# A planned kernel: a conversion leaves GpSimd, transfers on two queues are charged for each other, and sums in place go to the DMA queue

## The chip, the cores and the metric

The kernel runs on one core of a Trainium2 chip. The metric is the device time of one execution in microseconds; lower is better. The core has five engines with an instruction queue each: TensorE (PE, with its weight loads as PEld), VectorE (DVE), ScalarE (ACT), GpSimd (POOL) and SyncE (SP). In this kernel SP issues plain loads and stores, and POOL issues the transfers that add to their destination.

## The reference, cut to what matters

```
x = causal softmax attention of q, k, v     (2 batches, 12 heads, 448 rows, 64 columns)
h = x @ w_in    (896 x 768 @ 768 x 2048);  g = h * clip(h + 3, 0, 6) / 6;      y = g @ w_out
h = y @ w_in2                            ;  g = max(h, 0) + alpha * min(h, 0); out = g @ w_out2
```

Everything is float32 at the ends. The weights arrive as 64-bit words of float64.

## The kernel before, in words

**Arithmetic.** Each of the four large products is a Strassen form: seven block products where eight would be usual. A float32 product is made of three fp32r matmuls of 448 columns, from a high and a low part of each operand (`three`, L578). A layer has 168 such threes in `w_in` and 168 in `w_out`, so there are 672 in all, and `three` gives each of them a due time in the order of the program: 146.2 us plus 0.608 us for each one before it.

**Preparing operands.** `convert` turns one 768 KB load (`raw`) into 768 float32 columns: L249 on ACT takes the high words, a second pass (`lowest`) takes three low bits out of a byte, and L262 on DVE joins them. The second pass runs on ACT (L259), or, where `help` is set, on ACT or on POOL (L256). `help` is set for the first `HELP = 5` pairs of `w_in`. `split` (L275 to L284) and `both` (L612, L613) make the high part on ACT and the low part on DVE. Under `help` a split of attention's results may also go to POOL.

**Sums in place.** `add_on` adds one tile to another. It is either one DVE instruction (L303) or one DMA with an accumulating write issued by POOL (L301). There are 104 of them: in `w_in` two of 384 columns for each of 16 pairs; in `w_out` for each layer 12 of 768 columns (`onto`: four each for products 7, 6 and 3) and 24 of 448 columns (`add_g`: eight each for products 7, 6 and 4). The products of `w_out` run in the order 1, 2, 7, 6, 4, 5, 3. Sums for product 6 need those of product 7 to have been split, and those for 4 need the sums of 6.

**The order of the work** is found by a planner while the program is built (`Plan.solve`). It simulates the five queues with a cost for each operation, takes at each step the operation with the earliest due time among those that can start first, and writes the result out as a fixed order for each engine. Each engine then works strictly in that order, so one instruction that waits holds up everything behind it. A due time is worked back from the due times of the matmuls that need the result. An operation with two possible engines goes to the one that the planner thinks will be done first. A transfer is modelled by `lands(wait, us)`: it lands `us` after the later of its own wait and the transfer before it on the same queue (`landed[e]`). The two queues, SP's and POOL's, don't see one another. `raw` has three buffers, `ends` two, the weights' class `w` 20. `SEEDS` drive a random change of attention's due times; `SEND = 1` fixes one of the two sums of each `w_in` pair (the one into `w2`) on POOL.

**Stages.** Attention runs to about 90 us with the first preparation of weights beside it, then come `w_in` and `w_out` of layer 0, and from about 300 us those of layer 1.

Of the kernel before, what the change touches and what calls it, by code (L numbers as in the profile page):

```python
# [13 lines left out]
U8, U16, F16 = mybir.dt.uint8, mybir.dt.uint16, mybir.dt.float16  # L14
AF = mybir.ActivationFunctionType
ALU = mybir.AluOpType
# [6 lines left out]
PAIRS = KFF // 2  # L23
# [9 lines left out]
PE, DVE, ACT, POOL, SP = "PE", "DVE", "ACT", "POOL", "SP"  # L33


def f32(t):
    return t.bitcast(F32)
# [23 lines left out]

ISSUE, WAIT = 0.9, 4.2

TURN = {("r", "r"): 0.05, ("r", "t"): 0.17, ("r", "c"): 0.2, ("r", "q"): 0.15, ("r", "m"): 0.15, ("t", "r"): 0.12,
        ("t", "c"): 0.12, ("t", "q"): 0.1, ("m", "c"): 0.2, ("m", "r"): 0.1, ("m", "q"): 0.1}
LAG = {PE: 0.20, DVE: 0.12, ACT: 0.15, POOL: 0.10, SP: 0.04}
FAR = 1.0e6


class Plan:
# [3 lines left out]

    def op(self, on, emit, reads=(), writes=(), due=FAR, chain=None, also=(), port=False, mode=None):

# [24 lines left out]
    def solve(self, slots, strict, overlay, vary=0, seeds=()):  # L103
# [9 lines left out]
        bias = dict.fromkeys(LAG, 0.5)  # L113
        both = {o: o.on for o in self.ops[:vary]}
        hold = 0.01
        for i, seed in enumerate(seeds):
# [3 lines left out]
            if not i:  # L120
                hold = rng.choice((0.01, 0.05, 0.1, 0.2, 0.3, 0.5))
                bias = {e: rng.choice((0.0, 0.2, 0.5, 1.0, 2.0, 4.0)) for e in LAG}
# [9 lines left out]
        first = {}  # L132
        for o in self.ops:
            for b in o.bufs:
                if b.cls in strict:
                    first[b] = min(first.get(b, (FAR, 0)), (o.due, o.index))
        queue = {c: sorted((b for b in first if b.cls == c), key=first.get) for c in strict}
        waiting = {o: len(o.before) for o in self.ops}
        ready = {e: [] for e in LAG}
        clock, landed, port = dict.fromkeys(LAG, 0.7), dict.fromkeys(LAG, 0.0), 0.0  # L140

        def put(o):
            o.ready = {}
# [8 lines left out]
        while len(done) < len(self.ops):  # L152
            best = None
            room = {c: queue[c][:len(free[c])] for c in strict}
            for e in LAG:
                can = []
                for o in ready[e]:
                    t = max(clock[e] + TURN.get((mode, o.mode), 0.0) if e == PE else clock[e], o.ready[e])
                    if (e == POOL and e not in o.dma) or (e == DVE and o.port):
                        t = max(t, port)  # L160
                    ok = True
                    need = {}
                    for b in o.bufs:
                        if b.slot is None:
                            need[b.cls] = need.get(b.cls, 0) + 1
                            f = free[b.cls]
                            if len(f) < need[b.cls] or (b.cls in room and b not in room[b.cls]):
                                ok = False
                                break
                            t = max(t, sorted(f)[need[b.cls] - 1][0])  # L170
                    if ok and len(o.on) > 1:
                        def done_by(x, us):
                            late = max(clock[x], o.ready[x], port if (x == POOL and x not in o.dma) or (x == DVE and o.port) else 0.0)
                            return late + us + (bias[x] if x != o.on[0][0] else 0.0) + (sum(o.load) if x in o.dma else 0.0)

                        ok = e == min(o.on, key=lambda c: done_by(*c))[0]
                    if ok:
                        can.append((t, o))
                if can:
                    soon = min(can, key=lambda r: r[0])[0] + hold  # L180
                    t, o = min((r for r in can if r[0] <= soon), key=lambda r: (r[1].due, r[1].index))
                    key = (round(t, 2), o.due)
                    if best is None or key < best[0]:
                        best = (key, e, o, t)
            if best is None:
                raise RuntimeError("no step is possible: %s" % [
                    (e, o.on, [b.name for b in o.bufs]) for e in LAG for o in sorted(ready[e], key=lambda o: o.due)[:4]
                ])
            _, e, o, t = best
            for x, _ in o.on:  # L190
                ready[x].remove(o)
            o.eng, o.start = e, t
            mode = o.mode if e == PE else mode
            o.out = o.end = clock[e] = t + dict(o.on)[e]
            if (e == POOL and e not in o.dma) or (e == DVE and o.port):
                port = o.end
            if o.load and e in o.dma:
                first, us = o.load
                o.out = landed[e] = max(o.start + first, landed[e]) + us
            for b in [b for b in o.bufs if b.slot is None]:  # L200
                f = free[b.cls]
                k = min(range(len(f)), key=lambda i: f[i][0])
                b.slot = f.pop(k)[1]
                if b.cls in strict:
                    queue[b.cls].remove(b)
            for b in o.bufs:
                b.left -= 1
                b.end = max(b.end, o.out + LAG[e])
                if not b.left:
                    free[b.cls].append((b.end, b.slot))  # L210
            if any(b.cls in over_of for b in o.bufs):
                over_left -= 1
                over_end = max(over_end, o.end)
                if not over_left:
                    n = slots[over_cls]
                    free[over_cls] += [(over_end, n + i) for i in range(over_n)]
            for s in o.after:
                waiting[s] -= 1
                if not waiting[s]:
                    put(s)  # L220
            done.append(o)
# [3 lines left out]
class Kernel:  # L225
# [6 lines left out]

    def convert(self, src, sign=1.0, help=False, halves=False):

        nc, op = self.nc, self.plan.op
        raw = Buf("raw", "raw", 2 * DM, U32)
        w = Buf("w", "wf", DM, U32)
        ends = Buf("ends", "ends", DM, U32)  # L240
        keys = [(w, 0), (w, W3)] if halves else [w]

        def words(k):
            return raw.tile.rearrange("p (n two) -> p n two", two=2)[:, :, k]

        op((SP, 0.45), lambda e: nc.sync.dma_start(out=raw.tile, in_=src), writes=[(raw, "l"), (raw, "h")]).lands(2.3, 1.9)


        op((ACT, 0.80), lambda e: nc.scalar.activation(  # L249
            f32(w.tile), f32(words(1)), AF.Prelu, scale=sign * 2.0 ** -112, alpha=-2.0 ** 32), reads=[(raw, "h")], writes=keys)  # L250

        def lowest(e):
            byte = raw.tile.bitcast(U8).rearrange("p (n eight) -> p n eight", eight=8)[:, :, 3]
            if e == POOL:
                out = ends.tile.bitcast(U8).rearrange("p (n four) -> p n four", four=4)[:, :, 0]
                nc.gpsimd.tensor_scalar(out, byte, 1.0 / 32.0, 7.0, ALU.mult, ALU.min)  # L256
            else:
                out = ends.tile.bitcast(U16).rearrange("p (n two) -> p n two", two=2)[:, :, 0]
                nc.scalar.activation(out, byte, AF.Copy, bias=-0.4999, scale=1.0 / 32.0)  # L259

        op([(ACT, 0.93), (POOL, 0.95)] if help else (ACT, 0.93), lowest, reads=[(raw, "l")], writes=[ends])
        op((DVE, 0.87), lambda e: nc.vector.scalar_tensor_tensor(  # L262
            out=w.tile, in0=w.tile, scalar=3, in1=ends.tile.bitcast(U32), op0=ALU.logical_shift_left, op1=ALU.bitwise_or),
           reads=[ends], writes=keys, port=True)
        return w
# [29 lines left out]
    def add_on(self, out, cols, dst, src, reads, writes, send=False):  # L295

        nc = self.nc

        def emit(e):
            if e == POOL:  # L300
                nc.gpsimd.dma_start(out=dst(), in_=src(), accum_op=ALU.add)  # L301
            else:
                nc.vector.tensor_add(dst(), dst(), src())  # L303

        on = [(POOL, ISSUE), (DVE, 0.065 + 0.00105 * cols)]
        self.plan.op(on[:1] if send else on, emit, reads=reads, writes=writes, port=True).lands(WAIT, 0.0024 * cols, on=POOL)

    def copy(self, out, src, key, cols, sign=1.0):
        nc = self.nc
# [275 lines left out]

    def w_in(self, layer, m, src, due):
        nc, op = self.nc, self.plan.op
        help = layer * PAIRS + m < HELP
        w1 = self.convert(src[m], -1.0, help, True)
        w2 = self.convert(src[m + PAIRS], 1.0, help, True)  # L590
        s12 = Buf("w", "s12", DM, F32)
        left, right = slice(0, W3), slice(W3, DM)

# [1 line left out]
           reads=[(w2, 0), (w2, W3)], writes=[(s12, W3)], port=True)  # L595
        op((DVE, 0.47), lambda _: nc.vector.tensor_add(s12.tile[:, left], s12.tile[:, right], f32(w1.tile[:, left])),  # L596
           reads=[(s12, W3), (w1, 0)], writes=[(s12, 0)], port=True)
# [28 lines left out]
        a, b, c = Buf("ps", "a"), Buf("ps", "b"), Buf("ps", "c")  # L626
# [191 lines left out]
OVER = 38  # L818
WARM = 3
SPLIT = (0, 1)  # L820
HELP = 5
SEND = 1
SCALERS = 2
SEEDS = (16, 37982, 36857, 48248, 70450, 88331, 82478, 34058)
ATT = {"kq": 2 * S, "v": 8 * D, "e": 3 * P, "el": 4 * P, "small": 21, "a": 16 * P}


# [111 lines left out]
```

## Time and profile before

| What | us |
| --- | --- |
| median of three runs (523.89 to 526.14) | 523.96 |
| the profiled execution, its own time | 522.8 |
| its span, first to last instruction | 520.9 |
| busy: PE, DVE, ACT, POOL | 497.1 (95%), 448.0 (86%), 392.3 (75%), 117.3 (23%) |

The profile is of one execution on the one core. PE's busy time counts pipelined matmuls with modelled ends, so idle PE time in a stage is read from windows of that stage. A wait is put down to the releaser that came last. "Granted clock" is the share of TensorE's full clock that it was given.

### The profile page before, as it was taken

Reading aid. Unit: us, or ns where it says so; the run is one execution under the profiler, and the core shown is the slowest. Engines: PE = TensorE matmul, PEld = TensorE weight load, DVE = VectorE, ACT = ScalarE, POOL = GpSimd, SP = SyncE. Lnnn points to the kernel's source line nnn. Section 1 sums busy time; section 2 is a strip of 40 time slices with the busy share of each in tenths; the row PEclk is TensorE's granted clock in tenths of the full one; section 3 lists DMA queues with packets and bytes.
Section 4 is the critical chain, followed back from the end, with each engine's and each line's share of the span. In section 5 each row is a group of like instructions: output and inputs, shape, how many; then the busy total and the mean of one; then the engine's idle time right before and its main releaser. Section 6 shows DMA issues by size and latency. Waiting matters only on the chain. (4 is left out here: it accounts for less than half of the span.)

```text
span 520.9 us, 7558 instructions
## 1 busy us (share of the span) xinstructions
PE 497.1 (95%) x2598; PEld 428.7 (82%) x2598; DVE 448.0 (86%) x855; ACT 392.3 (75%) x746; POOL 117.3 (23%) x161
## 2 busy tenths in 40 slices
PE   8899999999799999997999999999999999879997
PEld 4666677788699999996999887999999999669996
DVE  6899998999699698988999999999879898699810
ACT  5999999687688798877875578888779997567201
POOL 2885687341100000351000001000000026010000
PEclk9999999999899999998999999999999999999999
DMA  8773115376654447899113255544446669930111
GB/s 276 271 240 110 52 42 182 94 208 160 171 147 138 170 140 246 205 227 250 30 57 94 108 137 155 152 136 137 137 137 185 200 196 227 205 61 1 53 54 53
DMA packets 23462, 76.10 MB, mean 146 GB/s; under 512 B 2688, under 2 KB 11264, under 8 KB 23424
## 3 DMA queue, kind: packets, MB, share of 16 engines
q1 hardware_dynamic: 15216, 61.76, 35.1%
q0 software_dynamic: 8208, 13.86, 15.3%
q8 instruction: 20, 0.33, 0.3%
q14 instruction: 18, 0.15, 0.1%
HBM read 59.00 MB, written 2.75 MB: 119 GB/s over the span
## 5 line engine op out<-in xcount | busy, mean ns | idle before, releaser
L259 ACT ACTIVATE ends<-raw 128x768 uint16<-128x768 uint8 x58 | 62.5, 1087 | 12.5 <-DMA raw<-w2o 4.3
L262 DVE SCALAR_TENSOR_TENSOR wf<-wf,ends 128x768 uint32<-128x768 uint32 x64 | 59.9, 953 | 12.6 <-ACT wf L249 12.5
L301 POOL DMA_DIRECT2D wf<-wf x24 | 21.0, 876 | 191.8 <-ACT ends L259 57.8
L249 ACT ACTIVATE wf<-raw 128x768 f32<-128x768 f32 x64 | 57.3, 904 | 2.0 <-DVE w3l L281 1.1
L301 POOL DMA_DIRECT2D g<-g x33 | 29.9, 1065 | 121.8 <-DVE g L657 29.0
L446 ACT ACTIVATE e<-e,small 128x384 f32<-128x384 f32 (+2 forms) x72 | 36.0, 505 | 7.3 <-DVE small L441 7.1
L441 DVE CUSTOM_DVE_ANT_0 e<-s,mask 128x384 f32<-128x384 f32 (+2 forms) x72 | 26.9, 417 | 4.3 <-PE s L490 4.2
L470 POOL TENSOR_SCALAR e<-e,small 128x128 f32<-128x128 f32 (+2 forms) x55 | 25.8, 486 | 8.2 <-DVE small L463 4.9
L313 ACT COPY o<-ya 128x448 f32<-128x448 f32 x3 | 1.6, 533 | 31.1 <-PE ya L578 31.1
L559 PE MATMUL o<-a,v 128*64 128x448 f32 (+3 forms) x192 | 23.4, 386 | 1.3 <-DVE small L441 0.9
L559 PEld LDWEIGHTS o<-a,v 128*64 128x64 f32 x192 | 12.5, 136 | 14.4 <-issue 4.6
L612 ACT CAST a1h<-wf 128x768 fp32r<-128x768 f32 x16 | 13.3, 833 | 11.8 <-DVE wf L262 11.8
L612 ACT CAST s<-wf 128x384 fp32r<-128x384 f32 x32 | 16.1, 511 | 8.1 <-DMA wf<-wf 8.1
L613 DVE TENSOR_TENSOR s<-wf,s 128x384 fp32r<-128x384 f32 x32 | 17.2, 552 | 5.4 <-ACT s L612 5.3
L256 POOL TENSOR_SCALAR ends<-raw 128x768 uint8<-128x768 uint8 x6 | 20.3, 3378 | 5.8 <-DVE wf L262 5.6
L490 PE MATMUL s<-kq 64*128 64x384 f32 (+2 forms) x144 | 20.5, 401 | 0.6 <-DMA kq<-kq 0.6
L515 PE MATMUL t<-ident,e 128*128 128x128 f32 x144 | 19.6, 279 | 1.5 <-POOL e L470 0.6
L490 PEld LDWEIGHTS s<-kq 64*128 64x128 f32 x144 | 13.3, 190 | 8.1 <-issue 3.6
L515 PEld LDWEIGHTS t<-ident,e 128*128 128x128 f32 x144 | 15.6, 141 | 4.5 <-POOL e L470 3.0
L612 ACT CAST s12h<-s 128x768 fp32r<-128x768 f32 x16 | 13.4, 836 | 7.6 <-DVE s L596 7.6
L613 DVE TENSOR_TENSOR s12l<-s,s12h 128x768 fp32r<-128x768 f32 x16 | 15.3, 955 | 2.7 <-PE a L578 2.1
L663 DVE SCALAR_TENSOR_TENSOR g<-r,alpha,g 128x448 f32<-128x448 f32 x24 | 16.3, 680 | 0.3 <-ACT r L661 0.3
(838 smaller groups left out, 1790.2 us busy)
## 6 DMA issues: line engine op xcount, KB each, us to landing
raw<-w1i SPq DMA_DIRECT2D x16, 768.0 KB, 5.7
raw<-w1o SPq DMA_DIRECT2D x16, 768.0 KB, 5.4
raw<-w2i SPq DMA_DIRECT2D x16, 768.0 KB, 4.7
raw<-w2o SPq DMA_DIRECT2D x16, 768.0 KB, 5.8
g<-g POOLq DMA_DIRECT2D x33, 224.0 KB, 7.0
kq<-kq SPq DMA_DIRECT2D x11, 448.0 KB, 5.9
v<-v SPq DMA_DIRECT2D x12, 256.0 KB, 2.7
wf<-wf POOLq DMA_DIRECT2D x16, 192.0 KB, 3.0
```

The source lines that it names most:

```text
L249: op((ACT, 0.80), lambda e: nc.scalar.activation(f32(w.tile), f32(words(1)), AF.Prelu, scale=sign * 2.0 ** -112, alpha=-2.0 ** 32), reads= ...
L259: nc.scalar.activation(out, byte, AF.Copy, bias=-0.4999, scale=1.0 / 32.0)
L262: op((DVE, 0.87), lambda e: nc.vector.scalar_tensor_tensor(out=w.tile, in0=w.tile, scalar=3, in1=ends.tile.bitcast(U32), op0=ALU.logical_s ...
L301: nc.gpsimd.dma_start(out=dst(), in_=src(), accum_op=ALU.add)
L441: nc.vector.tensor_tensor_reduce(out=view(), in0=t.tile[:, off:off + cols], in1=self.mask[:, at:at + cols], scale=-SCALE, scalar=3.0e38, o ...
L446: nc.scalar.activation(view(), view(), AF.Exp, bias=small.tile[:, u:u + 1], scale=-1.0, accum_out=small.tile[:, 7 + u:8 + u])
L470: (nc.gpsimd if e == POOL else nc.vector).tensor_scalar(view(), view(), by, 1.0, ALU.mult, ALU.mult)
L490: nc.tensor.matmul(t.tile[:, off:off + (i + 1) * P], lhsT=kq.tile[rows, S + i * P:S + (i + 1) * P], rhs=kq.tile[rows, 0:(i + 1) * P], star ...
L515: nc.tensor.transpose(t.tile[:, at * P:(at + 1) * P], src.tile[:, off:off + P], self.ident)
L559: nc.tensor.matmul(o.tile[side * D:(side + 1) * D, 0:cols], lhsT=v.tile[:, (2 * kc + side) * D:(2 * kc + side + 1) * D], rhs=a.tile[:, at: ...
L612: op((ACT, 0.07 + 0.00087 * cols), lambda _: nc.scalar.copy(out(0), src()), reads=keys, writes=[parts[0][0]])
L613: op((DVE, 0.065 + 0.00105 * cols), lambda _: nc.vector.tensor_sub(out(1), src(), f32(out(0))), reads=[*keys, parts[0][0]], writes=[parts[ ...
```

## The change

`convert` loses its `help`, so that the second pass always runs on ACT. In the planner, a transfer now begins at the latest of its own wait, the transfer before it on its own queue, and the last transfer on the other queue, the last of these counting for at most `SHARE` = 3.5 us (`lands_at`). The wait charged to an accumulating transfer depends on its columns: 2.2, 4.6 and 4.2 us for 384, 448 and 768, where it was 4.2 for all; its length is 0.0025 us a column instead of 0.0024. A sum in place goes to POOL whenever its landing there, plus the time of the sum on DVE, is at least `EARLY` = 3.0 us ahead of its due time; only otherwise is the faster one looked for. `SEND` becomes 0, and `SEEDS` are others.

```diff
-ISSUE, WAIT = 0.9, 4.2
+ISSUE, WAIT = 0.9, {384: 2.2, 448: 4.6, 768: 4.2}
...
+SHARE = 3.5
+EARLY = 3.0
+
+def lands_at(on, first, us, landed):
+    return max(first, landed[on], min(landed[POOL if on == SP else SP], first + SHARE)) + us
...
                             late = max(clock[x], o.ready[x], port if (x == POOL and x not in o.dma) or (x == DVE and o.port) else 0.0)
-                            return late + us + (bias[x] if x != o.on[0][0] else 0.0) + (sum(o.load) if x in o.dma else 0.0)
-
-                        ok = e == min(o.on, key=lambda c: done_by(*c))[0]
+                            late += bias[x] if x != o.on[0][0] else 0.0
+                            return lands_at(x, late + o.load[0], o.load[1], landed) if x in o.dma else late + us
+
+                        if POOL in o.dma and done_by(*o.on[0]) + o.on[-1][1] <= o.due - EARLY:
+                            ok = e == POOL
+                        else:
+                            ok = e == min(o.on, key=lambda c: done_by(*c))[0]
...
             if o.load and e in o.dma:
-                first, us = o.load
-                o.out = landed[e] = max(o.start + first, landed[e]) + us
+                wait, us = o.load
+                o.out = landed[e] = lands_at(e, o.start + wait, us, landed)
...
-    def convert(self, src, sign=1.0, help=False, halves=False):
+    def convert(self, src, sign=1.0, halves=False):
...
-        op([(ACT, 0.93), (POOL, 0.95)] if help else (ACT, 0.93), lowest, reads=[(raw, "l")], writes=[ends])
+        op((ACT, 0.93), lambda e: nc.scalar.activation(
+            ends.tile.bitcast(U16).rearrange("p (n two) -> p n two", two=2)[:, :, 0],
+            raw.tile.bitcast(U8).rearrange("p (n eight) -> p n eight", eight=8)[:, :, 3],
+            AF.Copy, bias=-0.4999, scale=1.0 / 32.0), reads=[(raw, "l")], writes=[ends])
...
-        self.plan.op(on[:1] if send else on, emit, reads=reads, writes=writes, port=True).lands(WAIT, 0.0024 * cols, on=POOL)
+        self.plan.op(on[:1] if send else on, emit, reads=reads, writes=writes, port=True).lands(WAIT[cols], 0.0025 * cols, on=POOL)
...
-        help = layer * PAIRS + m < HELP
-        w1 = self.convert(src[m], -1.0, help, True)
-        w2 = self.convert(src[m + PAIRS], 1.0, help, True)
+        w1 = self.convert(src[m], -1.0, True)
+        w2 = self.convert(src[m + PAIRS], 1.0, True)
...
-HELP = 5
-SEND = 1
+SEND = 0
-SEEDS = (16, 37982, 36857, 48248, 70450, 88331, 82478, 34058)
+SEEDS = (21, 95436, 61112, 3078, 26106, 52836, 96966, 84234)
```

## Rows read from the trace of the kernel before

**Rows 1.** Busy time by stage: window, PE PEld DVE ACT POOL, granted clock, DMA share, GB/s.
```profile
26.00:91.00 65.00, 62.80 (x476) 43.38 (x475) 60.74 (x199) 62.16 (x183) 47.51 (x67) 1.00 0.40 125
91.00:143.00 52.00, 46.61 (x215) 40.66 (x215) 45.55 (x74) 37.45 (x63) 14.27 (x13) 0.97 0.58 157
143.00:195.00 52.00, 52.00 (x258) 48.19 (x257) 46.94 (x76) 45.53 (x76) 3.23 (x4) 1.00 0.49 151
195.00:260.00 65.00, 61.56 (x295) 56.04 (x294) 58.61 (x87) 52.99 (x85) 14.22 (x17) 0.97 0.76 192
312.00:390.00 78.00, 77.20 (x375) 69.52 (x374) 69.98 (x114) 62.42 (x101) 6.08 (x7) 1.00 0.45 140
442.00:482.00 40.00, 34.70 (x166) 30.58 (x166) 35.29 (x52) 26.67 (x45) 3.31 (x4) 1.00 0.42 92
```

**Rows 2.** The same by 2 us, after a pause of PE.
```profile
136.00:138.00 2.00, 2.00 (x6) 1.78 (x6) 1.68 (x4) 2.00 (x4) 0.87 (x1) 0.50 0.00 0
138.00:140.00 2.00, 2.00 (x9) 1.79 (x8) 1.23 (x3) 0.73 (x2) 0.00 (x0) 0.74 0.72 132
```

**Rows 3.** Waits of PE, 95 to 521 us: total us, times, longest.
```profile
PE ya L578 <- DVE w6l L284: 6.0, 3, 2.5
PE a L578 <- ACT g L313: 4.2, 2, 3.9
```

**Rows 4.** Timelines of POOL and ACT: start, us, [idle before <- releaser].
```profile
125.65 0.86 POOL L301 DMA_DIRECT2D wf<-wf  x1 [8.33 <-PE a L578]
126.19 1.23 POOL L301 DMA_DIRECT2D g<-g  x1
...
134.63 0.51 ACT L612 CAST s<-wf 128x384 fp32r<-128x384 f32 x1 [3.89 <-DMA wf<-wf]
...
236.55 0.57 ACT L277 CAST x47h<-g 128x448 fp32r<-128x448 f32 x1 [1.00 <-DMA g<-g]
237.82 0.82 ACT L277 CAST w6h<-wf 128x768 fp32r<-128x768 f32 x1
```

**Rows 5.** The chain that ended last: start, us, what.
```profile
440.72 11.93 DMA g<-g
```

**Rows 6.** The second pass of the conversion on ACT and on POOL: busy, mean ns.
```profile
L259 ACT ACTIVATE ends<-raw 128x768 uint16<-128x768 uint8 x58 | 62.5, 1087 | 12.5 <-DMA raw<-w2o 4.3
L256 POOL TENSOR_SCALAR ends<-raw 128x768 uint8<-128x768 uint8 x6 | 20.3, 3378 | 5.8 <-DVE wf L262 5.6
```

**Rows 7.** The start of product 7 in layer 0, on PE's timeline.
```profile
223.04 0.36 PE L578 MATMUL yc<-x70h,w7h 128*128 128x448 f32 x1
```

**Rows 8.** Sums in place that ran on DVE, by shape, then by window.
```profile
L303 DVE TENSOR_TENSOR wf<-wf 128x768 f32<-128x768 f32 x16 | 15.3, 957 | 0.4
L303 DVE TENSOR_TENSOR g<-g,g 128x448 f32<-128x448 f32 x15 | 9.1, 618 | 0.0
L303 DVE TENSOR_TENSOR wf<-wf,s 128x384 f32<-128x384 f32 x16 | 8.9, 555 | 0.3
...
195.00:250.00 55.00, 10.04 (x12) 0.97 0.89 226
```

**Rows 9.** Sums that POOL issued as transfers: KB each, median us to landing.
```profile
g<-g POOLq DMA_DIRECT2D x33, 224.0 KB, 7.0
wf<-wf POOLq DMA_DIRECT2D x16, 192.0 KB, 3.0
wf<-wf POOLq DMA_DIRECT2D x8, 384.0 KB, 8.9
```

**Rows 10.** DMA from 195 to 250 us: by queue (packets, MB, share of 16 engines), then issues.
```profile
q0 software_dynamic: 2446, 4.56, 47.8%
q1 hardware_dynamic: 1440, 7.86, 41.3%
...
raw<-w2i SPq DMA_DIRECT2D x3, 768.0 KB, 5.8
wf<-wf POOLq DMA_DIRECT2D x4, 384.0 KB, 8.9
```

More of the change, by code (lines that the diff above doesn't have):

```diff
@@ L139, in solve @@
         ready = {e: [] for e in LAG}
-        clock, landed, port = dict.fromkeys(LAG, 0.7), dict.fromkeys(LAG, 0.0), 0.0
+        clock, landed, port = dict.fromkeys(LAG, 0.7), {SP: 0.0, POOL: 0.0}, 0.0
         def put(o):
@@ L250, in convert @@
             f32(w.tile), f32(words(1)), AF.Prelu, scale=sign * 2.0 ** -112, alpha=-2.0 ** 32), reads=[(raw, "h")], writes=keys)
[L252 to L259, printed above, removed]
-        op([(ACT, 0.93), (POOL, 0.95)] if help else (ACT, 0.93), lowest, reads=[(raw, "l")], writes=[ends])
+        op((ACT, 0.93), lambda e: nc.scalar.activation(
+            ends.tile.bitcast(U16).rearrange("p (n two) -> p n two", two=2)[:, :, 0],
+            raw.tile.bitcast(U8).rearrange("p (n eight) -> p n eight", eight=8)[:, :, 3],
+            AF.Copy, bias=-0.4999, scale=1.0 / 32.0), reads=[(raw, "l")], writes=[ends])
         op((DVE, 0.87), lambda e: nc.vector.scalar_tensor_tensor(
```

## The prediction

> **What bounds the kernel now.** I read the table of stages first. TensorE is the bound almost everywhere: from 143 to 195 us it is busy 52.00 of 52 us, and nothing that frees another engine can shorten such a stretch. What a new order can win is the time in which PE stands still. After attention that is 5.4 us from 91 to 143, 3.4 from 195 to 260, 0.8 from 312 to 390 and 5.3 from 442 to 482, 14.9 us together [rows 1]. In attention (26 to 91 us) PE is idle for 2.2 us, and ACT and DVE are nearly full as well (62.2 and 60.7 of 65 us).
>
> Two of the pauses have an aftermath. When PE comes back after the first one, its granted clock is 0.50 for 2 us and 0.74 for 2 more, with only 6 and 9 matmuls started [rows 2]; that is the lower of its two levels (1.2 of 2.4 GHz) for part of the time, and costs 2 x 0.50 + 2 x 0.26 = 1.5 us. The stage from 195 to 260 shows the same mean clock of 0.97 and a second such stretch, so I count it twice, 3.0 us. All pauses together are worth 14.9 + 3.0 = 17.9 us.
>
> Then the waits say who is late. PE waited 6.0 us in three pieces for the low part of product 6's weights, and 3.9 us once for a copy on ACT [rows 3]. Neither the copy nor the split is slow. ACT works in its written order, and stood in front of a transfer. The sum into `wf` issued at 125.65 us, beside another issued at 126.19, released ACT only at 134.63, after 3.89 us of idling; the copy that PE needed was behind it. In the second pause ACT waits for a `g` sum before x47h, an operand of product 4, while w6h, needed at once for product 6, comes only at 237.82 [rows 4]. In layer 1 the chain of the end runs through 11.93 us of one `g<-g` transfer [rows 5]. So the defect is an order that counts on transfers landing sooner than they do.
>
> **No conversion on GpSimd.** The second pass took 3378 ns on POOL in six cases and 1087 ns on ACT [rows 6]. It is removed from POOL (20.3 us) and added to ACT: 6 x 1.087 = 6.5 us. From 91 to 143 us ACT has 14.5 us free, from 26 to 91 only 2.8 [rows 1]. If half the six stay in the early part they are 3.3 us there, of which idling can hide 2.8 at best. POOL, relieved of 10 us, can take splits of attention in return. Bounds: 0 (all hidden or moved later) to 6.5 (all on the path). I take +1.5, near the lower end, since more than twice the needed room lies right behind.
>
> By the Trainium skill (GPSIMD Engine Reference, section Engine selection), a one-input elementwise operation on GpSimd runs roughly at line rate. By that rule POOL's pass would cost no more than ACT's, and moving it would gain nothing there; the trace differs, at three times ACT's time for this byte operation [rows 6], and the trace decides.
>
> **Sums as transfers.** The first three of product 7 has 216 threes before it, so its due time is 146.2 + 216 x 0.608 = 277.5 us; it began at 223.04 [rows 7]. Work runs some 54 us ahead of its due times, and a landing of under 10 us plus 3.0 us passes the new test nearly always. So I expect nearly all 47 sums that were on DVE to go to POOL, whatever their real urgency. DVE loses 15.3 + 9.1 + 8.9 = 33.3 us [rows 8]. As PE bounds the stages, this is worth nothing directly. What it costs: a sum on DVE took 0.56 to 0.96 us; as a transfer it lands 3.0 us (384 columns), 7.0 (448) or 8.9 (768) after its issue [rows 9]. POOL's issuing itself is small: 47 more at 0.86 us [rows 4] are 40 us, against the 404 us in which POOL was not busy. Queued behind a late sum are POOL's next sums, and on ACT the split that reads the result with everything written after it. Where sums begin early, as those of product 7 can during `w_in`, this is hidden by the distance to their product. SEND = 0 removes a compulsion of 16 sums that the test will send to POOL anyway: 0 us.
>
> The bandwidth is not free. From 195 to 250 us the POOL queue moved 4.56 MB in 47.8% of 55 us, 26.3 us of all 16 engines or 5.8 us per MB; SP's queue took 41.3%, 22.7 us for 7.86 MB or 2.9 per MB [rows 10]. That stretch held 12 of the sums on DVE, 10.04 us of them [rows 8]; only 8 of 768 columns and 4 of 448 make that time. As transfers they are 8 x 0.393 + 4 x 0.229 = 4.06 MB, 23.4 us. This makes 26.3 + 22.7 + 23.4 = 72.4 us of DMA in 55. What need not be there is the three loads of the next layer (2.36 MB, 6.8 us) and the four sums for product 3 (1.57 MB, 9.1 us); without them 56.5 us remain. The opening of `w_out` is thus just at capacity if the order is good.
>
> The Trainium skill (DMA: Bandwidth & Descriptors, section Issuing engines are not separate DMA queues) says that transfers of all issuing engines run on the same 16 DMA engines and interleave. This trace agrees, with 89% busy from two queues together [rows 10]; the rule speaks for charging queues for each other and against more sums on them. The same page (section Anatomy of one DMA) fits a transfer by 2.0 us plus its bytes at 436 GB/s. By that, as an estimate, a 448-column sum would land in 2.5 us and the 4.06 MB take 9.3 us, and there would be no overload, which would favour the third rival below; the 7.0 us of the row [rows 9] speak against it.
>
> **The planner's sharing.** With waits of 0.9 + 4.6 + 1.12 = 6.6 us for a 448-column sum, up to 3.5 more beside loads, the plan comes to 10.1 us; before it was 6.2. Median 7.0 us [rows 9] lies inside, the 11.93 us [rows 5] just outside. For 384 columns 4.1 to 7.6 us covers the median of 3.0, but not the 9 us from 125.65 to 134.63 [rows 4]. So splits on ACT should be placed after the work that PE needs. I take three quarters of the first pause with its slow clock (0.75 x 5.4 = 4.0 us), and half of the others, where the added transfers eat the rest: 2.5 of 4.9 (195 to 260), 0.4 of 0.8, 2.6 of 5.3. Bounds for the whole: none to all of 17.9 us, and a loss as in the first rival. Other seeds reorder attention: 0, between the 2.2 us that PE idles there and the same lost.
>
> **Sum.** 4.0 + 2.5 + 0.4 + 2.6 = 9.5 gained, 1.5 lost, net 8.0. From the profiled execution's 522.8 us this gives 514.8; the median of the runs lies 1.2 above it, so 516.0 us, 1.5% faster.
>
> **Rivals.**
> *The DMA engines become the bound in both openings of `w_out` (slower).* The rule begins sums for product 3 and loads for the next layer as soon as buffers allow, so the 72.4 us of transfers compete in 55. It decides as soon as over some 60 us must pass before product 4. For it: shares near full in that stretch already, ACT waiting for transfers there. Against it: 0.49 of the DMA is free from 143 to 195 us [rows 1], where product 7's sums and early loads fit. If half of the 17.4 us excess reaches PE in both layers, that is 17.4 lost; the other pauses still give 4.4, less 1.5 on ACT: 524.0 + 17.4 - 4.4 + 1.5 = 538 at worst, and with a quarter (8.7) 530. I call it 530, chance 0.28.
>
> *The waits only move (no change).* ACT still stands in front of some transfer: the sums that leave DVE bring new 3 to 9 us latencies, which eat what the better forecast gives, or the conversions on ACT hold attention up by up to 6.5 us. For it: 47 more results that ACT or DVE must wait for. 522 to 526 us, chance 0.20.
>
> *All pauses close.* With DVE free of 33.3 us and landings forecast right, PE runs through. 524.0 - 17.9 + 0 to 1.5 = 506 to 508 us, chance 0.10. Against it: the opening is at capacity.
>
> That the change does not do what it says (the test rarely true) is excluded by the 54 us of slack, except for sums whose chain is long; it is part of "only move".
>
> **How the numbers follow.** The forecast, 509 to 521 us, has 0.42. Half a per cent (2.6 us) is what a measurement here tells from none. Faster: 0.42 + 0.10 = 0.52; same 0.20; slower 0.28. The range goes from 507, nearly all pauses closed, to 530, the first rival's middle; below lies some 0.05, above 0.11. The forecast's own range is 509 to 521.
>
> **What would show it.** No L256 on POOL and 64 of L259 on ACT. L303 on DVE at a handful instead of 47, L301 near 104, DVE's busy time about 33 us lower. PE's pause near 132 us gone, with its slow clock. In the openings: DMA share at 0.9 or more over some 60 us; if then PE waits for w7 or w6 splits and ACT for `wf` or `raw` transfers in longer pieces than 2.5 us, the first rival holds. If PE idles more than 2.2 us between 26 and 91 us behind ACT, the conversions were mis-sized. I am wrong if the openings lose more than the present 8.7 us of PE with clock as before, or if a first pause remains.

## The result and the profile after

The changed kernel takes 519.62 us (median of 16 runs, 517.59 to 522.70); the kernel before, in 16 runs of its own, 526.18 (523.74 to 528.75). The ratio is 0.988 (95% interval 0.986 to 0.991): 1.2% faster. The median of before given above, 523.96, came from three of these runs, two of them at the quick end.

That matters for the traces. The changed kernel's profiled execution took 522.70 us, the slowest of its 16; that of before took 522.8, quicker than any of its 16 timed runs. The two spans are therefore the same, 520.8 and 520.9 us, and the two traces show where pauses lie, not how much was won. For the amount I go by the many runs.

Stages of the changed kernel, in the same columns and windows as [rows 1]:

```profile
26.00:91.00 65.00, 64.16 (x475) 43.43 (x472) 56.76 (x190) 63.10 (x182) 45.68 (x79) 1.00 0.36 114
91.00:143.00 52.00, 48.28 (x222) 43.53 (x221) 43.98 (x73) 39.57 (x64) 6.73 (x8) 0.93 0.55 164
143.00:195.00 52.00, 51.23 (x252) 46.84 (x251) 45.29 (x72) 46.04 (x76) 7.07 (x9) 1.00 0.66 183
195.00:260.00 65.00, 61.98 (x303) 56.21 (x302) 57.73 (x83) 53.35 (x86) 19.15 (x22) 1.00 0.85 217
260.00:312.00 52.00, 47.89 (x231) 43.63 (x230) 48.91 (x82) 34.52 (x56) 2.58 (x3) 0.98 0.33 97
312.00:390.00 78.00, 76.25 (x371) 69.53 (x370) 64.21 (x101) 61.42 (x99) 15.58 (x18) 0.99 0.67 173
442.00:482.00 40.00, 37.26 (x181) 33.88 (x182) 37.46 (x54) 30.58 (x51) 6.69 (x8) 1.00 0.57 123
```

The kernel before in the one window of these that [rows 1] leaves out:

```profile
260.00:312.00 52.00, 52.00 (x252) 46.73 (x251) 50.85 (x85) 34.10 (x55) 1.75 (x2) 1.00 0.33 99
```

Against [rows 1], PE in attention idles less (0.8 us instead of 2.2 from 26 to 91), the second opening loses 2.7 us instead of 5.3, and the first 3.0 instead of 3.4. But the pause after attention is still there (3.7 us of idling from 91 to 143 us instead of 5.4, at a mean clock of 0.93 instead of 0.97), and there are new ones from 260 to 312 us (4.1 us where there was none).

Transfers issued by POOL, as in [rows 9], and the sums left on DVE, as in [rows 8]:

```profile
g<-g POOLq DMA_DIRECT2D x48, 224.0 KB, 8.0
...
wf<-wf POOLq DMA_DIRECT2D x12, 384.0 KB, 8.1
...
wf<-wf POOLq DMA_DIRECT2D x14, 192.0 KB, 3.5
wf<-s POOLq DMA_DIRECT2D x11, 192.0 KB, 3.1
```
```profile
L311 DVE TENSOR_TENSOR wf<-wf x14: 547/958/960, 97.5 to 458.7; 128x768 f32<-128x768 f32 x12, 128x384 f32<-128x384 f32 x2
L311 DVE TENSOR_TENSOR wf<-wf,s x5: 557/558/559, 95.1 to 307.5; 128x384 f32<-128x384 f32 x5
```

So 85 of 104 sums are transfers (57 before); 19 stayed on DVE, 12 of 768 columns and 7 of 384. All of 448 columns went over.

The first large pause, on POOL's and ACT's timelines (compare [rows 4]), in PE's timeline and windows (compare [rows 2]), and the sum of such waits on ACT (total us, times, longest):

```profile
114.41 0.85 POOL L309 DMA_DIRECT2D wf<-wf  x1 [5.36 <-DVE s L601]
```
```profile
122.29 0.51 ACT L619 CAST s<-wf 128x384 fp32r<-128x384 f32 x1 [5.21 <-DMA wf<-wf]
```
```profile
129.69 0.74 PE L586 MATMUL a<-t200h,s12h 128*128 128x448 f32 x1 [3.72 <-ACT g L323]
```
```profile
126.00:128.00 2.00, 0.00 (x0) 0.00 (x0) 2.00 (x4) 2.00 (x5) 0.85 (x1) 1.00 0.36 58
...
130.00:132.00 2.00, 2.00 (x6) 1.79 (x6) 1.97 (x4) 1.51 (x3) 0.54 (x1) 0.50 1.08 281
132.00:134.00 2.00, 2.00 (x7) 1.75 (x7) 2.00 (x4) 1.45 (x4) 0.00 (x0) 0.50 1.01 349
134.00:136.00 2.00, 2.00 (x7) 1.79 (x6) 0.59 (x1) 1.87 (x2) 0.00 (x0) 0.55 0.32 60
```
```profile
ACT s L619 <- DMA wf<-wf: 13.4, 6, 5.2
```

A sum of 384 columns, issued at 114.41, releases ACT at 122.29, 7.9 us later. ACT stands before it for 5.21 us with a written order behind it, DVE waits for ACT in turn, and at 126 PE stops for 3.7 us. It then runs at the lower of its two clocks for almost 6 us, which costs another 2 x 0.50 + 2 x 0.50 + 2 x 0.45 = 2.9 us. Six such waits make 13.4 us on ACT in this execution; before the change there were five, 8.1 us, and a second execution of the changed kernel (e1 below) has 8.8. So this cause of pauses was not taken away; that it grew is not shown, though 25 of these sums are transfers now and 16 were. The change also planned them shorter: their wait went from 4.2 to 2.2 us.

The opening of `w_out`, 195 to 250 us, by queue as in [rows 10]:

```profile
q0 software_dynamic: 3255, 6.16, 61.3%
q1 hardware_dynamic: 1440, 7.86, 39.3%
```

The DMA engines are full there, as the prediction's sum put it, and yet PE loses no more than before. It loses more than it has to: in e8 below, where the two queues take 67% of this stretch, PE idles for 0.9 us from 195 to 260, here for 3.0.

### The profile page after: what moved, and what is told of

Same layout as the page of the kernel before. It is cut to its first block, busy times and chain, and to the rows that moved or that the text cites. A ratio compares the mean times of both kernels' runs of the same rounds, so it can differ in the third digit from the quotient of the medians.

```text
span 520.8 us, 7616 instructions
## 1 busy us (share of the span) xinstructions
PE 497.7 (96%) x2598; PEld 430.7 (83%) x2598; DVE 430.1 (83%) x816; ACT 397.4 (76%) x750; POOL 129.8 (25%) x196
## 5 line engine op out<-in xcount | busy, mean ns | idle before, releaser
L309 POOL DMA_DIRECT2D g<-g x48 | 42.0, 954 | 138.6 <-DVE g L670 43.1
L266 ACT ACTIVATE ends<-raw 128x768 uint16<-128x768 uint8 x64 | 68.5, 1085 | 4.4 <-DVE wf L270 3.5
L309 POOL DMA_DIRECT2D wf<-wf x26 | 23.5, 903 | 157.0 <-DVE s L601 54.0
L478 POOL TENSOR_SCALAR e<-e,small 128x384 f32<-128x384 f32 (+2 forms) x64 | 30.9, 520 | 8.7 <-DVE small L471 7.2
L619 ACT CAST s<-wf 128x384 fp32r<-128x384 f32 x32 | 16.1, 509 | 15.7 <-DMA wf<-wf 13.4
L567 PEld LDWEIGHTS o<-a,v 128*64 128x64 f32 x192 | 12.9, 136 | 14.4 <-ACT a L549 6.2
L498 PE MATMUL s<-kq 64*128 64x384 f32 (+2 forms) x144 | 23.1, 413 | 0.5 <-DVE small L449 0.2
L619 ACT CAST a1h<-wf 128x768 fp32r<-128x768 f32 x16 | 13.4, 835 | 10.4 <-DVE wf L270 10.4
L664 DVE SCALAR_TENSOR_TENSOR g<-r,g 128x448 f32<-128x448 f32 x24 | 14.9, 620 | 5.5 <-ACT r L662 5.1
L662 ACT ACTIVATE r<-g 128x448 f32<-128x448 f32 x24 | 13.7, 572 | 3.6 <-DVE g L652 3.5
## 6 DMA issues: line engine op xcount, KB each, us to landing
kq<-kq SPq DMA_DIRECT2D x11, 448.0 KB, 6.2
```

The lines of the kernel that those rows point to most:

```text
L266: op((ACT, 0.93), lambda e: nc.scalar.activation(ends.tile.bitcast(U16).rearrange("p (n two) -> p n two", two=2)[:, :, 0], raw.tile.bitcas ...
L478: (nc.gpsimd if e == POOL else nc.vector).tensor_scalar(view(), view(), by, 1.0, ALU.mult, ALU.mult)
L498: nc.tensor.matmul(t.tile[:, off:off + (i + 1) * P], lhsT=kq.tile[rows, S + i * P:S + (i + 1) * P], rhs=kq.tile[rows, 0:(i + 1) * P], star ...
L567: nc.tensor.matmul(o.tile[side * D:(side + 1) * D, 0:cols], lhsT=v.tile[:, (2 * kc + side) * D:(2 * kc + side + 1) * D], rhs=a.tile[:, at: ...
L619: op((ACT, 0.07 + 0.00087 * cols), lambda _: nc.scalar.copy(out(0), src()), reads=keys, writes=[parts[0][0]])
```

## The experiments

Each ratio is to the kernel before, in five rounds on the same chip, with its 95% interval. Two ways of cutting the change apart are used: keep a finished order and move only instructions to another engine at their place (e2, e3, e5), or change a rule and let the planner make a new order with the same seeds (the rest but e1). In the second way the order of attention shifts a little too, so a difference is that of a rule and of the one order that comes out with it. How far apart two equally good orders lie was not measured, and a small difference between two planned orders may be no more than that. The chips of e1 to e4, e5 to e8 and e9 to e12 differ, so runs of different groups are compared by their ratios.

**e1, the changed kernel again.**

> The changed kernel, unchanged, for a second trace and a comparison on the same chip as the next three. All theories: 0.988 of the kernel before (0.985 to 0.992). The theory that the remaining pauses come from sums of 384 columns that land late expects again one or more ACT waits of over 1.5 us in front of such a split, and PE pausing behind them; if the pauses sit elsewhere each time, it is chance.

520.55 us, ratio 0.989 (0.984 to 0.994). This execution's span is 517.1 us. The same pause sits at the same place, on ACT's timeline:

```profile
121.27 0.51 ACT L619 CAST s<-wf 128x384 fp32r<-128x384 f32 x1 [4.69 <-DMA wf<-wf]
```

It is not chance. The sum of these waits, however, differs from one execution to the next, and the lower clock lasts a shorter time here (windows after PE's pause):

```profile
ACT s L619 <- DMA wf<-wf: 8.8, 7, 4.7
```
```profile
128.00:130.00 2.00, 1.32 (x4) 1.20 (x5) 1.97 (x5) 1.14 (x3) 0.85 (x1) 0.62 0.97 285
130.00:132.00 2.00, 2.00 (x7) 1.79 (x6) 2.00 (x4) 1.89 (x4) 0.00 (x0) 0.52 1.10 334
```

**e2 and e3, order and engines crossed.** In e2 the order of before, with 32 sums and 6 conversions on the engines of after; in e3 the reverse. After the planner has written its order:

```diff
         for o in order:
+            if o.index in POOL_OPS:
+                o.eng = POOL
+            if o.index in DVE_OPS:
+                o.eng = DVE
+            if o.index in ACT_OPS:
+                o.eng = ACT
```

> The kernel before in its own order; only the six conversions run on ACT and the 32 sums in place that have another engine in the changed kernel run there (30 as transfers, 2 on DVE), each at its old place in the order. Theory order (the gain is the order, made with late landings in it): no gain, 1.00 to 1.02 of the kernel before, because the added transfers are waited for where a DVE sum was. Theory engines (a relieved DVE and POOL give the gain): 0.985 to 0.993.

> The changed kernel in its own order; the six conversions go back to POOL at their places and the 32 sums back to the engines of the kernel before. Theory order: keeps most of the gain, 0.986 to 0.994. Theory engines: loses it, 0.998 to 1.01. Each POOL pass of 3.4 us instead of 1.1 should cost at most some 1 us in attention if its place is not urgent.

e2: 576.52 us, 1.093 (1.088 to 1.099). e3: 532.34 us, 1.011 (1.006 to 1.015). Neither theory had e2; e3 lies at the upper end of the theory of engines (0.998 to 1.01). The new engines in the old order cost 9%; ACT's waits of e2 show why:

```profile
ACT s L612 <- DMA wf<-s: 38.2, 11, 7.1
...
ACT x64h L277 <- DMA g<-g: 11.4, 2, 6.4
ACT x62h L277 <- DMA g<-g: 8.6, 2, 4.3
```

A sum that becomes a transfer where a DVE instruction stood is waited for at once. But the new order without its engines loses too. Order and engines belong to each other, and neither alone carries the gain.

**e4, sums of 384 columns on DVE.**

```diff
         on = [(POOL, ISSUE), (DVE, 0.065 + 0.00105 * cols)]
+        if cols == W3:
+            on = on[1:]
```

> The changed kernel, planned again with all 32 sums of 384 columns on DVE (25 were transfers); the others as before. Theory order-but-384-too-optimistic (the pauses left are ACT waiting for these transfers, some 13 us of waits in the profile): 2 to 6 us faster than the changed kernel, ratio 0.976 to 0.985, and no ACT wait for such a transfer. Theory engines: DVE has 14 us more to do, 0.988 to 0.995. Rival: the pauses move to other waits, 0.986 to 0.990.

509.19 us, 0.967 (0.963 to 0.971); on this chip the changed kernel took 520.55. So 11.4 us hung on planning 25 sums as transfers of 192 KB, about twice the 2 to 6 us that the first theory named. The stage after attention is whole, at full clock, though DVE has more to do:

```profile
91.00:143.00 52.00, 51.63 (x253) 47.08 (x253) 51.52 (x88) 45.37 (x75) 3.61 (x4) 1.00 0.58 178
```

**e5, conversions back on POOL.** The order of the changed kernel; the six conversions run on POOL at their places (the method of e2).

> The changed kernel in its own order, with only the six conversions back on POOL at their places (that they cost 3.4 us each there and not 1.1 is not planned for). Theory conversions (the loss of e3, between 91 and 143 us, comes from them): 1.005 to 1.012 of the kernel before, PE under 42 us busy in that stage. Theory sums (it comes from the sums put back): 0.987 to 0.993, as the changed kernel.

527.70 us, 1.004 (1.002 to 1.007). The changed kernel stands at 0.988, so the six passes are worth 1.6%, about 8 us, in this order, which counts on ACT for them; what e3 lost beyond e5, 0.6%, is left for the sums, and the intervals overlap. PE is busy 43.44 us from 91 to 143, not quite under the 42 that I named. POOL's timeline, three waits from 91 to 143 us and the windows:

```profile
95.41 6.95 POOL L270 TENSOR_SCALAR ends<-raw 128x768 uint8<-128x768 uint8 x2
```
```profile
PE a L592 <- DVE g L658: 3.5, 1, 3.5
ACT r L668 <- DVE g L658: 7.0, 5, 5.5
DVE wf L276 <- POOL ends L270: 2.9, 1, 2.9
```
```profile
92.00:96.00 4.00, 2.67 (x13) 2.07 (x12) 2.05 (x3) 0.00 (x0) 3.85 (x3) 1.00 0.27 71
96.00:100.00 4.00, 1.84 (x8) 1.74 (x9) 4.00 (x7) 3.17 (x5) 3.92 (x2) 0.94 0.43 146
100.00:104.00 4.00, 4.00 (x14) 3.60 (x14) 3.96 (x7) 3.00 (x6) 3.27 (x2) 0.63 0.70 201
```

POOL is the one engine that is full throughout from 92 to 100 us. DVE waits for its pass, ACT for the sum that DVE has behind it, and PE, for 3.5 us, for the next such sum; it gets 4.5 us of work in 8. The rest of PE's 8.6 us of idling in this stage is the old pause behind a 384 sum (5.1 us at 131.5), which the conversions don't explain.

**e6, the kernel before with 384 sums on DVE.** The edit of e4, in the kernel before.

> The kernel before, planned again by its own rules with the 32 sums of 384 columns on DVE (16 were transfers). Theory that late 384 sums are most of what either kernel loses: 0.975 to 0.985, PE's pause of 3.9 us behind such a sum gone, the pauses in the openings of w_out left. Theory that the change's other parts matter as much: 0.988 to 0.995. Rival, an order made for POOL's short conversions keeps the loss: 0.995 to 1.005.

517.70 us, 0.986 (0.983 to 0.990). Between the first two theories. PE's pause behind such a sum is gone, the pauses of the openings stay (3.3 us from 195 to 260, 3.9 from 442 to 482): the kernel before loses 8 us to planning 16 transfers of this kind.

```profile
91.00:143.00 52.00, 51.13 (x250) 46.39 (x249) 51.77 (x88) 42.77 (x71) 3.65 (x5) 1.00 0.52 156
```

**e7, no sharing.**

```diff
-    return max(first, landed[on], min(landed[POOL if on == SP else SP], first + SHARE)) + us
+    return max(first, landed[on]) + us
```

> The changed kernel, planned without the other queue in a landing time (SHARE has no effect); waits by columns, the early rule and the seeds stay. The orders of PE and SP are the same, those of ACT and DVE differ. Theory sharing: it keeps ACT from standing in front of late transfers, so without it 0.993 to 1.01. Rival, it changes too little: 0.985 to 0.991, as the changed kernel.

534.85 us, 1.020 (1.017 to 1.023). The rival falls, and the loss is larger than the theory named: 3.2% against the changed kernel. ACT's waits:

```profile
ACT s L619 <- DMA wf<-wf: 20.9, 10, 6.6
...
ACT ends L266 <- DMA raw<-w1o: 5.2, 3, 3.1
ACT s L619 <- DMA wf<-s: 5.2, 7, 1.5
```

Without sharing 29 sums of 384 columns are transfers, not 25. So sharing works in two ways, by what ACT is put in front of and by which sums go over; the two were not measured apart.

**e8, no early rule.**

```diff
-                        if POOL in o.dma and done_by(*o.on[0]) + o.on[-1][1] <= o.due - EARLY:
+                        if False:
```

> The changed kernel, planned without the early rule: 47 sums are transfers instead of 85, of 384 columns only 6 instead of 25. Theory early sums (they take work off DVE in time): slower than the changed kernel, 0.993 to 1.005. Theory 384 (the rule sends the wrong sums, those of 384 columns): faster than the changed kernel, 0.970 to 0.985, near e4 if the early sums of 448 columns are worth nothing.

505.19 us, 0.962 (0.959 to 0.965). That is more than the second theory named. The early rule does harm: without it the same change gives 3.8%, not 1.2%. The page's busy times, PE's longest waits from 30 us on, and three stages:

```profile
PE 490.3 (98%) x2598; PEld 426.5 (85%) x2598; DVE 446.0 (89%) x855; ACT 397.9 (79%) x751; POOL 95.0 (19%) x156
```
```profile
PE ya L586 <- DVE w6l L292: 1.4, 3, 0.6
PE ya L586 <- DVE y L772: 1.3, 1, 1.3
```
```profile
91.00:143.00 52.00, 51.76 (x256) 47.65 (x255) 51.76 (x88) 45.71 (x75) 3.46 (x4) 1.00 0.59 182
143.00:195.00 52.00, 52.00 (x259) 48.20 (x258) 50.09 (x80) 48.95 (x79) 5.17 (x6) 1.00 0.61 179
195.00:260.00 65.00, 64.08 (x315) 58.76 (x314) 61.67 (x91) 53.03 (x85) 10.48 (x12) 1.00 0.57 149
```

DVE is nearly full from 91 to 143 (51.76 of 52), and PE is as well: that costs it nothing.

**e9, no early rule and 384 sums on DVE.** The edits of e4 and e8.

> The changed kernel, planned without the early rule and with all 32 sums of 384 columns on DVE (e8 had 6 of them as transfers); 41 sums stay transfers. Theory 384 (each such transfer is a risk): a little faster than e8, 0.955 to 0.963 of the kernel before. Theory early rule (beyond the 384 sums, its early 448 and 768 sums cost too): faster than e4, which differs from it only by the rule for these, so below 0.965; if the rule is harmless for them it equals e4 at 0.967.

504.35 us, 0.960 (0.956 to 0.964). Its interval covers e8's value, so the last six transfers of 384 columns can't be told from none. It lies under e4, which differs from it by the early rule for sums of 448 and 768 columns: those early sums cost some 0.7% as well, with intervals that just meet. This is the quickest kernel of the study, if by nothing that can be told from e8.

**e10, neither early rule nor sharing.** The edits of e7 and e8.

> As e8 (no early rule), and also without the other queue in a landing time. What is left of the change is the conversion on ACT, the waits by columns and the seeds. Theory sharing (it matters by itself): 0.980 to 0.995, well above e8's 0.962. Theory that sharing only mends what the early rule does: 0.960 to 0.970, as e8.

517.16 us, 0.985 (0.981 to 0.988). Sharing matters by itself, 2.3% between e10 and e8. What it prevents, among ACT's waits (e8 has neither; 10 sums of 384 columns are transfers here, 6 there):

```profile
ACT x67h L285 <- DMA g<-g: 8.8, 2, 4.4
ACT s L619 <- DMA wf<-wf: 7.4, 4, 4.3
```

**e11, a longer wait for 384 columns.**

```diff
-ISSUE, WAIT = 0.9, {384: 2.2, 448: 4.6, 768: 4.2}
+ISSUE, WAIT = 0.9, {384: 5.2, 448: 4.6, 768: 4.2}
```

> The changed kernel, planned with a wait of 5.2 us instead of 2.2 for a sum of 384 columns (23 instead of 25 of them are transfers; the order of ACT differs). Theory wait (the change's 2.2 us is too short, so ACT stands in front of these transfers): 0.972 to 0.983. Theory transfers (their landing varies too much for any wait, or ACT's order leaves no better place): 0.985 to 0.990, as the changed kernel, with waits for such a sum on ACT as long as there.

509.92 us, 0.971 (0.967 to 0.974). 23 of these sums are still transfers, and 9 to 10 us come back by a number alone. ACT's waits for them shrink, from 13.4 us in the one execution of the changed kernel and 8.8 in the other, to

```profile
ACT s L619 <- DMA wf<-wf: 2.5, 2, 1.7
```

So not the transfers as such, but a forecast that is too short for them: with 5.2 us planned, the kernel can't be told from the one with the same sums on DVE (e4, 0.963 to 0.971).

**e12, the kernel before with all conversions on ACT.** `HELP = 0` in the kernel before, planned again.

> The kernel before, planned again by its own rules with HELP = 0, so that all conversions run on ACT and nothing else of the change is made. Theory conversions (POOL's 3.4 us passes hold up attention and the first pairs; worth some 1.6% as between e5 and the changed kernel): 0.980 to 0.990. Theory that this is worth something only in the new order: 0.995 to 1.005.

519.04 us, 0.987 (0.983 to 0.991). From 91 to 143 us PE is busy 50.66 us, where it was 46.61 [rows 1]. One part of the change alone gives as much as the whole. Where the gain comes from is not shown. No engine waits for one of the six passes in the trace of before, and what is gone here is the pause of 3.9 us behind a 384 sum [rows 3]: ACT's longest wait for such a sum is 1.9 us in this order, where it was 3.89 [rows 4]. PE's stage and these waits:

```profile
91.00:143.00 52.00, 50.66 (x245) 45.44 (x244) 48.99 (x82) 42.69 (x70) 9.05 (x10) 1.00 0.66 185
```
```profile
ACT s L612 <- DMA wf<-wf: 5.7, 6, 1.9
```

## Why the prediction came out right, and where its steps were wrong

The forecast was 1.5% faster and 516.0 us, measured are 1.2% and 519.62 us, of which some 2 us are the quick three runs that the sum began from. But the small net is made of large parts, and several of mine were wrong and cancelled: that the sum came out is in good part luck. From before to after, along e12, e10, e8 and the changed kernel: conversions -1.3%, the waits by columns, SEND, the seeds and the landing time by which an engine is chosen -0.2% together (not to be told from none), sharing -2.3%, the early rule +2.7%. The large ones hold along another path too: sharing gives 3.2% between e7 and the changed kernel, and the early rule costs 3.5% between e10 and e7. By the prediction's own last test it was wrong in one thing: a first pause remains.

- *What bounds the kernel.* Held. PE was the bound, and ACT's standing before late transfers made its pauses: shown for the first one by e6 and e4, argued from the waits for those in the openings. e8 with its short waits shows that most of them could go: its span of 502.6 us is 18.3 under that of before, and of this 11.5 us are PE's idle time (23.8 to 12.3) and 6.8 its busy time (497.1 to 490.3), in which the matmuls at the slow clock are contained.
- *No conversion on GpSimd, taken as 1.5 us lost.* Wrong in sign. I counted the engine that receives the work (ACT, 6.5 us) and let POOL's relief count for splits only. e12 measures 6.6 us won (525.59 to 519.04). In the new order each pass's own length counts, 3.4 us instead of 1.1 in the chain to DVE, ACT and PE: e5 loses 3.5 us of PE at one place by it. In the kernel before no wait shows this, though its plan counted on 0.95 us, and whether e12's gain is due to the passes or to the other order stays open.
- *The test of the early rule nearly always true, all 47 sums moved.* Wrong. I took the due times to start at 146.2 us. This base is 9.0 + 2 x 6 x 5.8 - 2.0 = 76.6 us; I had put 12 in place of the 6 pairs of heads (and the text on the kernel above has the same wrong figure). Product 7 is thus due at 207.9 us and starts 15 us after that, not 54 ahead [rows 7]. The due time in the test is moreover that of the sum's start: the planner takes the transfer's own time off it. 30 sums went over and 2 came back, not 47, and DVE's busy time fell from 448.0 to 430.1 us, not by 33.
- *The moved sums cost nothing but part of the openings' gain.* The size was wrong, and the place. They cost 14 us (e8 against the changed kernel, 2.7%). In the traces e8 does 41 matmuls more from 91 to 195 us; at the plan's 0.608 us for three that is some 8 of the 18 us between the two spans; the rest comes later. The greater part goes through sums of 384 columns: I had noted that the plan's 4.1 to 7.6 us did not cover the 9 us of the trace [rows 4], and yet priced the pause behind it as three quarters gone, 4.0 us of the sum. It stayed, with 3.7 us of idling in one execution and 3.2 in the other. e11 and e4 show that term by itself, 9 to 11 us. The early rule does most of its harm together with the wait of 2.2 us: with 5.2 and the rule (e11) the kernel is at 0.971, 0.9% above e8.
- *The planner's sharing, 9.5 us gained.* Right in mechanism, near in size: e10 to e8 gives 12 us. By stages it did not come as priced, since the first pause stayed, and the plan's landing times were read wrongly. The planner counts a landing from the start of the issue, without the 0.9 us, so a 448 sum has 5.7 to 9.2 us in the new plan and 5.3 in the old (not 6.6 to 10.1 and 6.2), and a 384 sum 3.2 to 6.7 (not 4.1 to 7.6). The old plan gave the 384 sum 5.1: for the very sums behind the first pause, the new forecast is shorter unless a load or an earlier sum is charged to them.
- *The first rival, DMA as the bound in the openings.* The transfers did fill that stretch, 100% from both queues, and it did not become a loss: PE's idling went from 3.4 to 3.0 and from 5.3 to 2.7 us. By the Trainium skill (DMA: Bandwidth & Descriptors, section Issuing engines are not separate DMA queues), transfers of all issuers interleave on the same engines; here the trace agrees, with 61.3% and 39.3% from the two queues. The order bore it, though e8, with 67% there, idles 2.1 us less from 195 to 260; whether the fuller DMA is the reason was not tested.
- *The second rival, waits that only move.* It is the nearest to what the trace shows: new pauses from 260 to 312 us, the old one behind another 384 sum. The early rule's loss is of this kind; it took 2.7 of 3.8%, not all.

What stays open: the 192 KB sum's landing varies from some 3 us in the median to nearly 8 and 9 in the two pauses, and no run measured by itself which part is the loads beside it. In the changed kernel's trace two loads of 768 KB are issued from 110 to 124 us, and SP's queue takes 33.9% of the DMA engines in that time, the sum 14.4%.

## What to carry to other kernels

In a static order, what counts is not how long a transfer takes in the median but whether an in-order engine is placed in front of it too soon: forecast the landing with its neighbours, and be generous, since one late sum cost a whole pause of TensorE and the slow clock after it. Moving work off an engine that is not the bound gains nothing by that engine's busy time, and what it does to the latency of each step counts: DVE busy for over 99% of a stage was harmless, while its sums as transfers were waited for. When a change has several parts, measure them alone: here the other parts won 3.8% together and the early rule gave back 2.7%, and the net looked like a modest success.

## What the runs showed of the hardware that was not expected

- The byte pass over 128 x 768 takes 3378 ns on GpSimd, written as a multiplication and a minimum into bytes, and 1087 on ScalarE, written as a scaled copy into 16-bit words [rows 6].
- Accumulating transfers inside the core's memory used 5.8 us of all 16 DMA engines per MB, plain loads 2.9 [rows 10]; the accumulating ones landed 3.0 to 8.9 us after their issue in the medians by size [rows 9].
- After a pause of 3.7 us the granted clock was 0.50 to 0.55 for almost 6 us in one execution of the changed kernel, after one of 3.2 us 0.52 to 0.62 for some 3 in another (e1), after one of 3.9 us 0.50 and 0.74 for some 3 in the kernel before. By those clocks the aftermath cost 1.5 to 2.9 us on top of the pause, an estimate.
